# A Mamba-2 scan and a GELU MLP on one NeuronCore: two units share one stretch of scan matmuls, inter-chunk output in 32x64 tiles, stage 1 in 512 columns

## The chip, the cores and the metric

The kernel runs on one core of one Trainium2 chip. The metric is the device time of one execution in microseconds (us). Three runs of the kernel before are given. The profile is one further execution, recorded instruction by instruction.

The engines are named as the profile does: PE is TensorE (matmul), PEld its weight loads, DVE VectorE, ACT ScalarE, POOL GpSimd, and SPq the queue of SyncE, which here issues nearly all DMAs.

## The reference

There are 4 sequences (batch) of 8 heads, 768 tokens, head dimension 32 and state size 16. The scan is computed in chunks; the result goes token by token (3072 tokens of 256 features) through a two-layer MLP.

```python
cum = np.cumsum(log_a, axis=-1)                       # within a chunk
M = einsum('bhin,bhjn->bhij', C, B) * exp(cum_i - cum_j) * causal
y_intra = einsum('bhij,bhjd->bhid', M, x)
y_inter = einsum('bhin,bhnd->bhid', C, state) * exp(cum)
y = y_intra + y_inter
state = exp(sum log_a) * state + sum_j exp(cum_last - cum_j) * B_j x_j
...
h = y.reshape(3072, 256) @ w_in                       # 256 -> 2048
g = 0.5 * h * (1 + tanh(c * (h + 0.044715 * h**3)))
out = g @ w_out                                       # 2048 -> 256
```

## The kernel before

The kernel uses chunks of 128 tokens: 6 for each sequence, 24 in all (`gc`). Two chunks make a unit `u` of 256 tokens, so there are 12 units, three for each sequence. Inputs are cast to bf16, and the decays are folded into B and C ahead of the matmuls, so `bh` is the scaled B transposed (16 state rows of 8 heads, 128 partitions), `ch` the scaled C transposed, and `ce` two copies of `ch` in which the odd or the even heads are zeroed.

For each unit the program has these steps, by the names that the order uses:

- `G` (L614): C·B for all head pairs of both chunks, 8 matmuls in 32-row by 128-column tiles of the PE array, into the PSUM tiles `ga` and `gb`. `M.u.0` and `M.u.1` (L627) multiply them by the causal mask on DVE.
- `D` (L644): the chunk's contribution to the state, 16 matmuls in 128x32 tiles of 64 columns each (8 where a chunk is the last of its sequence). `S` (L692) adds it to the decayed state, `SP` (L704) makes a bf16 copy `sp_new` spread over a block diagonal. Both are on DVE.
- `Y` (L657): the output, 128x32 tiles, 128 columns. A chunk takes 8 matmuls for the inter-chunk part (L673, `sp_new` times `ce`; the first chunk of a sequence has none) and 8 for the intra-chunk part (L682). `yev` copies it to `xm` in SBUF, by ACT or DVE.
- `s1.u.i` (L723): stage 1 of the MLP in 8 steps, each 4 matmuls of 256 columns (two blocks of 128 features, contraction 256 in two halves) into one PSUM bank. `gelu.u.i` on ACT takes it into `gT`.
- `s2.u.k.q` (L740): stage 2 for chunk `k` in four steps of 4 matmuls of 256 columns each. `oev` copies the result out of PSUM, `store` sends it to memory.

PSUM has eight banks: two each for `ga` and `gb`, one for `yb` (Y), one for `o_ps` (stage 2), two for `hp` (stage 1, `D`, small things), taken in turn.

There is no scheduler at work in the build: the string `ORDERED` is the order in which all steps are issued, and each engine runs its own part of it in that order. A suffix `:A`, `:D`, `:P` names the engine of a step that can run on several. From unit 3 on, `Y.u`, `D.u+1` and `G.u+1` are one step. `~n` are warm-up matmuls on zeros.

Loads: `x` by unit (`load_x`, cast by `castx`), B and C by sequence (`load_bc`, scaled by `mul`). Sequence 0 is laid out by steps of its own. Sequence 1 is transposed on PE (`T`, `N`). Sequences 2 and 3 go through memory: `load_wr` writes the scaled bf16 values, `load_tr` reads them back transposed (`bh`, `ch`), `load_bn` reads them plain; `F` makes `ce` from `ch`. The lines of interest of the DMA queue are L170 (`load_bc`), L177 (`load_x`), L513 (`load_wr`), L520 (`load_tr`), L525 (`load_bn`) and L760 (`store`). All DMAs but the first few loads of `a` follow each other on SPq in the written order.

Of the kernel before, what the change touches and what calls it, by code (L numbers as in the profile page):

```python
# [8 lines left out]
FP32 = mybir.dt.float32  # L9
# [5 lines left out]
XL = 6  # L15
# [15 lines left out]
s2.0.0.1.o wo.2.0 wo.2.1:D s1.2.2 gelu.2.1 s2.0.1.1.o D.3 G.3 S.3.0 gelu.2.2 s1.2.3 gelu.2.3 S.3.1
M.3.0 M.3.1 load_wo.3 load_x.4 wo.3.0:A s2.0.0.2.o s2.0.1.2.o wo.3.1 SP.6 s1.2.4 s1.2.5 castx.4.None
s2.0.0.3.o s2.0.1.3.o gelu.2.4 gelu.2.5 oev.0:D s1.2.6 Y.3 oev.1 yev.3.0.2:D s2.1.0.0.o s2.1.0.1.o
s2.1.0.2.o gelu.2.6 s2.1.0.3.o s1.2.7 S.4.0 oev.2 recip.3 S.4.1 s1.3.0 s2.1.1.0.o M.4.1 s2.1.1.1.o
gelu.3.0 s2.1.1.2.o gelu.2.7 s2.1.1.3.o s1.3.1 s1.3.2 gelu.3.1 gelu.3.2 oev.3:D s2.2.0.0.o
s2.2.0.1.o s1.3.3 gelu.3.3 s2.2.0.2.o load_bc.2.1 load_bc.2.0 s2.2.0.3.o mul.2.1:P s1.3.4 M.4.0
load_x.5 s1.3.5 gelu.3.4 mul.2.0:P castx.5.None:D SP.7 oev.4:D SP.8 SP.9 s2.2.1.0.o s2.2.1.1.o
gelu.3.5 s2.2.1.2.o s1.3.6 s2.2.1.3.o gelu.3.6 Y.4 load_wr.2.1 s1.3.7 oev.5:D s2.3.0.0.o yev.4.0.2
load_x.6 load_wr.2.0 S.5.0 gelu.3.7 s1.4.0 s2.3.0.1.o M.5.0 load_tr.2.1 gelu.4.0 SP.10 M.5.1 s1.4.1
s2.3.0.2.o castx.6.None s1.4.2 load_bn.2 gelu.4.1 load_tr.2.0 s1.4.3 store.0 s2.3.0.3.o gelu.4.2  # L40
s1.4.4 gelu.4.3 store.2 F.2 load_x.7 oev.6:D Y.5 s2.3.1.0.o S.6.0 gelu.4.4 yev.5.0.2:D S.6.1
s2.3.1.1.o s1.4.5 gelu.4.5 s2.3.1.2.o load_bc.3.1 s2.3.1.3.o store.1 oev.7 s1.4.6 s1.4.7 s2.4.0.0.o
mul.3.1 load_bc.3.0 store.3 gelu.4.6 load_x.8 castx.7.None load_wr.3.1 gelu.4.7 s2.4.0.1.o s1.5.0
store.4 gelu.5.0 s1.5.1 load_x.9 s2.4.0.2.o M.6.1 M.6.0 gelu.5.1 SP.12 s2.4.0.3.o s1.5.2 oev.8:D
mul.3.0 castx.8.None gelu.5.2 s1.5.3 gelu.5.3 s2.4.1.0.o Y.6 S.7.0 load_wr.3.0 yev.6.0.2 s1.5.4
s2.4.1.1.o gelu.5.4 S.7.1 SP.13 s1.5.5 s2.4.1.2.o s2.4.1.3.o gelu.5.5 oev.9:D SP.15 s1.5.6 s1.5.7
# [38 lines left out]
def kernel(  # L85
# [32 lines left out]
    AL = 2 * Q  # L118

# [8 lines left out]
    GT_BUFS = 5  # L128
# [873 lines left out]
```

## Time and profile before

| | |
|---|---|
| three runs | 116.52, 116.56 (median), 116.89 us |
| span of the profiled execution, first to last instruction | 115.0 us |
| time of the profiled execution itself | not recorded beside its span; the median of the runs is 1.56 us above the span |
| busy: PE, PEld, DVE, ACT, POOL | 108.1, 91.7, 68.0, 70.0, 25.9 us |
| granted PE clock | 1.000 |
| DMA | 16.00 MB, 139 GB/s over the span |

The span is the part of the time that the engines' instructions cover. What lies around it is start and end of the execution. A busy PE is not the same as a PE at its peak, since matmuls overlap: the profile gives each a duration of 0.2 to 0.3 us, while ends follow each other every 0.11 us. Rates are therefore read from the chain of waits, which lists by how much each group pushed the end on, and not from the busy time.

### The profile page before, as it was taken

Reading aid. Unit: us, or ns where it says so; the run is one execution under the profiler, and the core shown is the slowest. Engines: PE = TensorE matmul, PEld = TensorE weight load, DVE = VectorE, ACT = ScalarE, POOL = GpSimd, SP = SyncE. Lnnn points to the kernel's source line nnn. Section 1 sums busy time; section 2 is a strip of 40 time slices with the busy share of each in tenths; the row PEclk is TensorE's granted clock in tenths of the full one; section 3 lists DMA queues with packets and bytes.
Section 4 is the critical chain, followed back from the end, with each engine's and each line's share of the span. In section 5 each row is a group of like instructions: output and inputs, shape, how many; then the busy total and the mean of one; then the engine's idle time right before and its main releaser. Section 6 shows DMA issues by size and latency. Waiting matters only on the chain.

```text
span 115.0 us, 3377 instructions
## 1 busy us (share of the span) xinstructions
PE 108.1 (94%) x1421; PEld 91.7 (80%) x1421; DVE 68.0 (59%) x136; ACT 70.0 (61%) x133; POOL 25.9 (23%) x54
## 2 busy tenths in 40 slices
PE   6979888999999999999999999999999999999990
PEld 2235566888879997989989899889898898999970
DVE  6889998989974755969448491186750851010100
ACT  3159687687654455747675876456495576758620
POOL 7636856806439020201120030000000000000000
PEclk9999999999999999999999999999999999999999
DMA  0999979979994779997556922350003020001113
GB/s 24 231 309 336 332 212 191 317 132 321 215 238 101 141 177 203 196 272 175 88 131 150 209 62 85 111 86 0 0 9 134 0 71 26 0 0 55 42 62 120
DMA packets 43103, 16.00 MB, mean 139 GB/s; under 512 B 36688, under 2 KB 41552, under 8 KB 43088
## 3 DMA queue, kind: packets, MB, share of 16 engines
q1 hardware_dynamic: 42896, 15.70, 55.3%
q8 instruction: 11, 0.18, 0.7%
q10 hardware_dynamic: 192, 0.09, 0.3%
q14 instruction: 4, 0.03, 0.1%
HBM read 11.07 MB, written 3.93 MB: 130 GB/s over the span
## 4 chain that ended last, share of the span: by engine, by line
PE 82%; DVE 5%; DMA 4%; SPq 3%; issue 2%; ACT 2%; DVEq 0%
PE hp L732 35%; PE o_ps L750 34%; DMA x_t<-in_x_dram 4%; PE yb L750 3%; PE yb L673 3%; PE ga L618 2%; PE yb L682 2%; DVE m L628 1%; DVE sp_new L706 1%; SPq L164 1%; ACT gT L736 1%; SPq L151 1%; SPq L160 1%; DVE rt L364 1%; DVE r_t L354 1%
## 5 line engine op out<-in xcount | busy, mean ns | idle before, releaser
L736 ACT ACTIVATE gT<-hp 128x512 bf16<-128x512 f32 x96 | 54.3, 596 | 28.9 <-PE hp L732 28.6
L732 PE MATMUL hp<-xm,w_in_sb 128*128 128x256 bf16 x384 | 53.4, 273 | 1.1 <-DVE s_new L699 0.5
L750 PE MATMUL o_ps<-w_out_sb,gT 128*128 128x256 bf16 x352 | 46.8, 273 | 0.0
L732 PEld LDWEIGHTS <-w_in_sb 128*128 128x128 bf16 x384 | 41.2, 114 | 4.0 <-issue 2.7
L750 PEld LDWEIGHTS <-gT 128*128 128x128 bf16 x384 | 37.4, 98 | 4.1 <-issue 0.4
L341 DVE COPY o_sb<-o_ps 128x256 f32<-128x256 f32 x12 | 5.1, 425 | 26.9 <-PE o_ps L750 26.9
L628 DVE TENSOR_TENSOR m<-ga,tri 128x1024 bf16<-128x1024 f32 x12 | 14.6, 1216 | 0.0
L628 DVE TENSOR_TENSOR m<-gb,tri 128x1024 bf16<-128x1024 f32 x11 | 13.4, 1216 | 0.0
L339 POOL CAST x<-x_t 128x512 bf16<-128x512 f32 x8 | 6.0, 756 | 28.1 <-DMA x_t<-in_x_dram 24.4
L706 DVE SCALAR_TENSOR_TENSOR sp_new<-s_new,pend,bmask 128x256 bf16<-128x256 f32 x17 | 8.0, 483 | 0.1
L699 DVE SCALAR_TENSOR_TENSOR s_new<-s_new,pend,hp 128x64 f32<-128x64 f32 x13 | 3.5, 272 | 7.4 <-PE hp L651 7.3
L720 PE MATMUL yb<-wz 128*128 128x512 bf16 (+2 forms) x21 | 6.6, 455 | 1.1 <-DVE warm L226 1.1
L337 ACT ACTIVATE o_sb<-o_ps 128x256 f32<-128x256 f32 x10 | 3.8, 383 | 5.1 <-PE o_ps L750 3.8
L682 PE MATMUL yb<-m,x 128*32 128x128 bf16 x192 | 6.1, 220 | 0.0
L337 ACT ACTIVATE xm<-yb 128x512 bf16<-128x512 f32 x8 | 4.8, 596 | 1.3 <-PE hp L651 0.7
L720 PEld LDWEIGHTS <-wz 128*128 128x128 bf16 x21 | 2.3, 116 | 4.1 <-issue 2.1
L673 PE MATMUL yb<-ce,sp_new 128*32 128x128 bf16 x160 | 5.3, 221 | 0.0
L339 POOL CAST w_out_sb<-wf 128x512 bf16<-128x512 f32 x6 | 4.1, 692 | 4.7 <-DMA wf<-in_moe_w_out_dram 4.7
L618 PE MATMUL ga<-ce,bh 32*128 32x256 bf16 x48 | 4.7, 273 | 0.3 <-DVE par L289 0.3
L618 PE MATMUL gb<-ce,bh 32*128 32x256 bf16 x48 | 4.7, 273 | 0.0
L750 PE MATMUL yb<-w_out_sb,gT 128*128 128x256 bf16 x32 | 4.5, 273 | 0.0
L682 PEld LDWEIGHTS <-x 128*32 128x32 bf16 x192 | 3.7, 96 | 0.9 <-issue 0.9
(114 smaller groups left out, 75.0 us busy)
## 6 DMA issues: line engine op xcount, KB each, us to landing
out_dram<-o_sb SPq DMA_DIRECT2D x24, 128.0 KB, 2.0
x_t<-in_x_dram SPq DMA_DIRECT2D x20, 128.0 KB, 3.9
wf<-in_moe_w_in_dram SPq DMA_DIRECT2D x4, 512.0 KB, 7.0
wf<-in_moe_w_out_dram SPq DMA_DIRECT2D x4, 512.0 KB, 7.1
bc_t<-in_C_dram SPq DMA_DIRECT2D x3, 384.0 KB, 4.7
bc_t<-in_B_dram SPq DMA_DIRECT2D x3, 384.0 KB, 5.7
scr<-bc SPq DMA_DIRECT2D x4, 192.0 KB, 2.3
x_t<-in_x_dram SPq DMA_DIRECT2D x1, 512.0 KB, 4.4
```

What stands on the lines that cost most here:

```text
L337: nc.scalar.activation(o, i, AF.Copy)
L339: nc.gpsimd.tensor_copy(out=o, in_=i)
L341: nc.vector.tensor_copy(out=o, in_=i)
L618: nc.tensor.matmul(out=gbank(g)[:, 256 * k:256 * k + 256], lhsT=bh_of(2 * u + k)[gs], rhs=ce_of(2 * u + k)[gs], start=True, stop=True, til ...
L628: nc.vector.tensor_tensor(out=m_of(u)[:, 2 * i:2 * i + 2].rearrange("p g k e t -> p (g k e) t"), in0=gx[i].rearrange("p g (k t) -> p (g k) ...
L673: nc.tensor.matmul(out=y4[32 * j:32 * j + 32, k, w], lhsT=sp[:, 32 * h:32 * h + 32], rhs=ce_of(gc)[:, h % 2], start=first(j), stop=False, ...
L682: nc.tensor.matmul(out=y4[32 * j:32 * j + 32, k, w], lhsT=X16[u][:, k, 32 * h:32 * h + 32], rhs=m[:, h // 2, h % 2, :], start=first(j), st ...
L706: nc.vector.scalar_tensor_tensor(out=sp_new.rearrange("p (g d) -> p g d", g=4), in0=(XN[0][:, H * D:H * D + 64] if gc == 0 else state[("s" ...
L720: nc.tensor.matmul(out=t[:, 0:m * 128], lhsT=wz, rhs=w3.to_broadcast([128, m, 128]), start=True, stop=True, skip_group_check=True)
L732: nc.tensor.matmul(out=hp[:, j * T:(j + 1) * T], lhsT=w_in_k[:, w, q, k], rhs=xm[:, w, u * T:(u + 1) * T], start=(w == 0), stop=(w == 1))
L736: nc.scalar.activation(gts[u][:, 2 * i:2 * i + 2], hps.pop((u, i)).rearrange("p (j t) -> p j t", j=2), AF.Gelu_apprx_tanh)
L750: nc.tensor.matmul(out=ops[gc], lhsT=gts[u][:, fi, k * Q:(k + 1) * Q], rhs=w_out_sb[:, fi, :], start=(fi == 0 and (u > 0 or k == 0)), stop ...
```

## The change

1. **Two units, one stretch.** From unit 4 on, `Y` is divided into `Yi` (intra, 128x32 tiles) and `YI` (inter), and units 4-5, 6-7, 8-9 and 10-11 each run them together: `Yi.u Yi.u+1`, then `YI.u YI.u+1`, with the `D` of the next two units and the `G` of one of them beside. The `G` of odd units (5, with `D.5`; 7, 9, 11) stands alone between MLP steps. Each pair's output fills two whole banks, one for each half of the features; `yew` copies them to `xm`, one on ACT and one on DVE.
2. **Inter Y in 32x64 tiles.** `YI` takes 4 matmuls for a chunk instead of 8: contraction 32 (two heads of 16 states), 64 output rows, unmasked `ch`. Tiles 0 and 1 write the two halves of one bank, tiles 2 and 3 those of another. From unit 6 on `G` is in 32x64 tiles too, 16 matmuls instead of 8.
3. **Stage 1 in 512 columns.** From unit 4 on one step takes one block of 128 features for both units: 2 matmuls of 512 columns in place of 4 of 256. `gT` has two buffers for a pair each.
4. **Banks by step.** The four banks a, b, o and y may each hold stage 1, stage 2, `D` or Y; `@` in the order names them.
5. **GpSimd held.** `hold.4` is a copy of one column of `sp_new` of chunk 4 on GpSimd, which stands ahead of `mul.1.1` there.
6. **A new order** of all steps from `Y.0` on, engines of some copies included; some dependencies of `load_tr`, `load_bn` and `mul` are stated more narrowly.

The built instruction lists show it so: PE has 2566 instructions (matmuls and weight loads, with one branch) instead of 2838.

```diff
 ORDERED = """
...
-load_x.5 s1.3.5 gelu.3.4 mul.2.0:P castx.5.None:D SP.7 oev.4:D SP.8 SP.9 s2.2.1.0.o s2.2.1.1.o
-gelu.3.5 s2.2.1.2.o s1.3.6 s2.2.1.3.o gelu.3.6 Y.4 load_wr.2.1 s1.3.7 oev.5:D s2.3.0.0.o yev.4.0.2
...
+castx.2.None:P bn1:D s1.1.0 SP.3
+recip.1 ce1.0:A G.2 D.2 gelu.1.0 s1.1.1 gelu.1.1 S.2.0 SP.4 s1.1.2 wo.0.0:P s2.0.0.0 gelu.1.2 M.2.1
+load_bc.1.1 s1.1.3 gelu.1.3 hold.4 s2.0.1.0 load_bc.1.0 mul.1.1:P M.2.0 s1.1.4 s1.1.5 load_wo.1 load_x.3
+mul.1.0:P gelu.1.4 gelu.1.5 Y.2 s1.1.6 T.1.0 s1.1.7
...
+gelu.3.2 G.5 load_tr.2.1 gelu.3.3 D.5 SP.8 s2.2.0.1 S.5.0 s1.3.4
...
+load_bn.2 s1.3.5 s1.3.6 oev.4:A castx.6.None:D load_tr.2.0 load_bc.3.1 SP.10 load_bc.3.0 s2.2.1.0@o
+s2.2.1.1 gelu.3.5 M.5.1 F.2 s1.3.7 load_x.8 s2.2.1.2 gelu.3.6 gelu.3.7 Yi.4@ya Yi.5 YI.4 YI.5 D.6@b D.7
+G.6 yew.4.0 yew.4.1 s2.2.1.3 S.6.0 S.6.1 S.7.0 s1.4.0@a S.7.1 s2.3.0.0@y gelu.4.0 M.6.0 s1.4.1@b s1.4.2@a
+oev.5:A mul.3.1:D gelu.4.1 gelu.4.2 s1.4.3@o gelu.4.3 s2.3.0.1 s2.3.0.2 s1.4.4@a s1.4.5@b gelu.4.5
+s2.3.0.3 gelu.4.4 s1.4.6@o gelu.4.6 M.6.1 G.7 mul.3.0:P oev.6:D SP.12 castx.8.None:P s1.4.7@b s1.4.8@a
+SP.14 M.7.0 s2.3.1.0@o gelu.4.7 gelu.4.8 s1.4.9@b s1.4.10@y gelu.4.9 load_wr.3.1 s2.3.1.1 load_wr.3.0
+gelu.4.10 s1.4.11@b s1.4.12@a store.3 load_x.9 s2.3.1.2 M.7.1 s1.4.13@y load_tr.3.1 load_bn.3 load_tr.3.0
+load_x.10 s2.3.1.3 gelu.4.11 gelu.4.12 oev.7:D castx.9.None:A s1.4.14@a store.7 gelu.4.13 s1.4.15@b
+s2.4.0.0@o s2.4.0.1 gelu.4.14 load_x.11 gelu.4.15 SP.13 Yi.6@ya Yi.7 D.8@b D.9 G.8 YI.6 YI.7 yew.6.0
...
+gelu.6.15 s2.6.0.1 Yi.8@ya Yi.9 D.10@b D.11 YI.8 YI.9 G.10
...
+gelu.8.15 Yi.10@ya Yi.11 YI.10 YI.11 yew.10.0
...
-s2.11.0.2.yb s2.11.0.3.yb s2.11.1.0.o s2.11.1.1.o s2.11.1.2.o store.19 s2.11.1.3.o oev.22 oev.23
-store.22 store.21 store.18 store.23
+s2.11.0.2 s2.11.1.0@b s2.11.1.1 s2.11.1.2 store.19 s2.11.1.3 store.21 s2.10.0.1
+s2.10.0.2 oev.23:D s2.11.0.3 store.23 s2.10.0.3 oev.20:A store.18 store.20 oev.22:A store.22
 """
...
+    def f_hold(c):
+        nc.gpsimd.tensor_copy(out=held, in_=state[("sp", c)][:, 0:1])
+
     def f_G(u):
+        if u > U2 + 1:
+            for k in range(2):
+                for i, g in [(i, g) for i in range(2) for g in range(4)]:
+                    gs, js = slice(32 * g, 32 * g + 32), slice(64 * i, 64 * i + 64)
+                    nc.tensor.matmul(out=gbank(g)[js, 256 * k:256 * k + 256], lhsT=bh_of(2 * u + k)[gs, js],
+                                     rhs=ce_of(2 * u + k)[gs], start=True, stop=True,
+                                     tile_position=(32 * g, 64 * i), skip_group_check=True)
+            return
...
+    def f_Yi(u):
+        v = u % 2
+        YT[u] = (take("y"), take("o")) if v == 0 else YT[u - 1]
+        for w, k, j in [(w, k, j) for w in range(2) for k in range(2) for j in range(4)]:
+            h, t = 4 * w + j, v * T + k * Q
+            nc.tensor.matmul(out=YT[u][w][32 * j:32 * j + 32, t:t + Q],
+                             lhsT=X16[u][:, k, 32 * h:32 * h + 32], rhs=MT[u][:, h // 2, k, h % 2],
+                             start=(v == 0 and k == 0), stop=True, tile_position=(0, 32 * j), skip_group_check=True)
+
+    def f_YI(u):
+        for k in range(2):
...
+            for g in range(4):
+                gs, i = slice(32 * g, 32 * g + 32), g % 2
+                nc.tensor.matmul(out=YT[u][g // 2][64 * i:64 * i + 64, t:t + Q],
+                                 lhsT=sp[gs, 64 * g:64 * g + 64], rhs=ch_of(gc)[gs], start=False, stop=True,
+                                 tile_position=(32 * g, 64 * i), skip_group_check=True)
+
+    def f_yew(u, w, eng):
+        copy(eng, xm[:, w, u * T:u * T + PT], YT[u][w])
...
+        else:
+            q, k = divmod(i, 4)
             for w in range(2):
...
+                nc.tensor.matmul(out=hp, lhsT=w_in_k[:, w, q, k], rhs=xm[:, w, u * T:u * T + PT],
+                                 start=(w == 0), stop=(w == 1))
```

More of the change, by code (lines that the diff above doesn't have):

```diff
@@ L41 @@
[L41 to L46, printed above, removed]
@@ L322, with take @@
     gx = [ps1.tile([128, 2, 512], FP32, name=f"g{i}") for i in "ab"]
[L323 removed]
+    bank = {k: ps1.tile([128, 512], FP32, name=f"bank_{k}") for k in "aboy"}
+    yb = bank["y"]
+    at = []
+    hp_turn = []
+    def take(pool):
+        if at:
+            return bank[at.pop(0)]
+        if pool == "hp":
+            hp_turn.append(0)
+            return bank["ba"[len(hp_turn) % 2]]
+        return bank[pool]
     y4 = yb.rearrange("p (c w t) -> p c w t", c=2, w=2)
```

262 lines of the change are left out of this document (145 added, 117 removed).

## The prediction

> **What bounds the kernel now.** I read the page's slices first, then the busy time in stretches, then the chain of waits in order of time.
>
> ```profile
> 20.70:49.66 28.96, 28.96 (x380) 25.64 (x383) 22.04 (x38) 17.64 (x32) 10.24 (x12) 1.00 0.90 206
> 49.66:111.94 62.28, 62.26 (x804) 56.02 (x804) 27.93 (x48) 38.96 (x73) 2.60 (x3) 1.00 0.31 77
> 111.94:115.00 3.06, 0.00 (x0) 0.00 (x0) 0.00 (x0) 0.38 (x1) 0.00 (x0) 1.00 0.37 130
> ```
>
> After the stretch come its length and the busy time of PE, PEld, DVE, ACT and POOL, then granted clock, DMA share and GB/s. From 20.70 to 111.94 us PE is never idle, at full clock, while DVE and ACT have room, above all in the second half. So only PE work taken away there shortens the kernel; ahead of it lies a head of 20.7 us, behind it a tail of 3.06 us. The chain (start, us added to the end, what) gives the true price of PE work, at its end and around unit 5:
>
> ```profile
> 108.87 1.31 PE yb L750 x12
> 110.18 1.76 PE o_ps L750 x16
> 111.94 0.02 issue
> 111.96 0.38 ACT o_sb L337
> ```
>
> ```profile
> 49.22 0.44 PE hp L732 x4
> 49.66 0.23 PE yb L673 x8
> 49.88 0.11 PE yb L682 x8
> 49.99 0.11 PE yb L673 x8
> 50.11 0.11 PE yb L682 x8
> 50.22 0.06 PE hp L651 x8
> 50.28 0.21 PE ga L618 x2
> 50.49 0.01 PE gb L618 x2
> 50.50 0.10 PE ga L618 x2
> 50.60 0.01 PE gb L618 x2
> 50.61 0.98 PE o_ps L750 x8
> ```
>
> Twelve MLP matmuls of 256 columns add 1.31, so 0.1092 each and 0.437 for a step of four. Eight Y matmuls in 128x32 tiles add 0.113 by their starts: two rounds of four side by side, 0.057 a round. `D` takes 0.06, `G` two rounds of 0.11. Each time the shape of the tiles changes, about 0.115 comes on top: 0.23 for the first eight of Y, 0.21 for the first of G, 0.98 instead of 0.87 on the way back. Y, D and G take 1.06 us together, and 0.34 of it are three changes of shape.
>
> **Part by part: inter Y.** Y.4 to Y.11 have 16 chunks, two of them (12 and 18, first of their sequences) without an inter part. For 14 chunks two rounds (0.113) become four matmuls in 32x64 tiles. If the four run side by side that is one round, and 14 x 0.057 = 0.79 us is saved. That row tiles overlap shows here:
>
> ```profile
> 9.68 0.20 PE L596 MATMUL o_ps<-x4b,bc0s 32*32 32x64 bf16 x1
> ...
> 9.80 0.19 PE L596 MATMUL hp<-x4b,bc0s 32*32 32x64 bf16 x1
> ```
>
> These are the first and the last of 32 matmuls of 64 columns, over two groups of rows and four of columns, all started within 0.12 us, 4 ns apart. But there different row groups write different banks, while in `YI` tiles 0 and 1 share one. No row shows that. The bounds: one round saves 0.79; two rounds (tile 1 beside tile 2) save nothing; four one after the other cost 14 x (0.227 - 0.113) = 1.59 - 0.79 more, so a loss of 0.79. I take one round, by the nearest row: other rows and other columns of the array. The Trainium skill, "TensorEngine Tiling (Array Packing)", section "Gotcha 1: PSUM Pressure", says that different row tiles cannot access the same PSUM bank at once; by that the saving is lost or reversed. Its page "PSUM — Partial Sum Buffer" (Terms, Quadrant) reports that different 32-partition quadrants of one bank may be accessed at the same time, which speaks for one round.
>
> **Changes of shape**, counted from Y.3 on. Before: eight stretches of three, and Y.11 with two: 26. After: G.4-Y.3-D.4 three; G.5-D.5 three; the stretch of units 4-5 five (into Yi, YI, D, G, back, since D stands between YI and G); those of 6, 8 and 10 three each; G.7, G.9 and G.11 two each: 26. So the sharing itself saves nothing. G in 32x64 tiles has twice the tiles of half the width, still two rounds: nothing, or up to 0.11 a unit (six units, 0.66) if 16 weight loads don't keep up; at the 4 ns above they do.
>
> **512 columns.** 256 matmuls become 128.
>
> ```profile
> 9.92 1.09 PE L720 MATMUL yb<-wz 128*128 128x512 bf16 x5
> ```
>
> ```profile
> L720 PE MATMUL yb<-wz 128*128 128x128 bf16 x1 | 0.2, 219 | 0.0
> ```
>
> These five are four of 512 columns and one of 128: (1.09 - 0.219) / 4 = 0.218 us each, against 2 x 0.1092 = 0.2184. The row is good to some 0.0025 each, so 128 of them give a gain of 0.05, between a gain of 0.35 and a loss of 0.25. I take 0.05. The weight loads that go were hidden under matmuls.
>
> **The head.**
>
> ```profile
> 19.68 0.62 POOL L339 CAST x<-x_t 128x512 bf16<-128x512 f32 x1 [0.68 <-DMA x_t<-in_x_dram]
> ...
> 21.46 1.50 POOL L499 TENSOR_TENSOR bc<-bc_t,pt 128x768 bf16<-128x768 f32 x1 [0.39 <-DVE sp_new L706]
> ```
>
> ```profile
> 20.70 0.60 PE L732 MATMUL hp<-xm,w_in_sb 128*128 128x256 bf16 x4
> ...
> 24.90 0.50 PE L508 MATMUL ga<-ident,bc 128*128 128x128 bf16 x6
> ```
>
> The new order moves G.1 ahead of stage 1 and puts small DVE steps and casts otherwise. Yet by s1.1.1 (20.70) the same PE steps have to be done, and D.2 just before it needs castx.2, whose load lands at 19.68 in the same queue order: no change, 0.2 either way. `hold.4` stands on POOL ahead of mul.1.1, mul.1.0, wo.1.0 and castx.3, and T.1.0 on PE (24.90) waits for both muls. But mul.1.1 was released by an sp_new before too, at 21.46. Now mul.1.0 takes POOL's 1.50 after it: 21.5 + 3.0 = 24.5. Cost nothing; with SP.4 later than 21.9, that lateness.
>
> **The tail.**
>
> ```profile
> 6.32 0.72 ACT L337 ACTIVATE ce<-hp 128x256 bf16<-128x256 bf16 x2 [3.08 <-PE hp L449]
> ```
>
> ```profile
> 110.67 2.03 SPq L760 DMA_DIRECT2D out_dram<-o_sb  x4
> ```
>
> Before, one eviction (0.38) and one store follow the last matmul. After, s2.10.0.3 is last; `oev.20` waits for it, and `oev.22`, whose matmuls ended 0.44 earlier, is queued behind it on ACT. Two evictions in a row take 0.72 (the row of two of 256 columns), so the last store is released 0.34 later, and its issue (2.03 / 4 = 0.5) falls some 0.1 behind that of store.20. Cost 0.45, between 0.34 and 0.6.
>
> **What is late next.** With PE full, the rest of the order is worth nothing unless something arrives late. Evictions fit: behind `YI` PE has G and at least 0.44 of stage 2 before s1 needs `xm`, and `yew` is of a gelu's size. The tightest is sequence 3.
>
> ```profile
> L736 ACT ACTIVATE gT<-hp 128x512 bf16<-128x512 f32 x96 | 54.3, 596 | 28.9 <-PE hp L732 28.6
> ```
>
> ```profile
> 41.66 1.23 SPq L520 DMA_TRANSPOSE bh<-scr  x1
> ...
> 48.62 2.61 SPq L177 DMA_DIRECT2D x_t<-in_x_dram  x2
> ...
> 60.95 0.57 SPq L525 DMA_DIRECT2D bn<-scr  x1
> ```
>
> ```profile
> x_t<-in_x_dram SPq DMA_DIRECT2D x20, 128.0 KB, 3.9
> ...
> bc_t<-in_B_dram SPq DMA_DIRECT2D x3, 384.0 KB, 5.7
> ```
>
> D.9 now stands in the stretch of units 6-7. At 50.61, 64 MLP steps were done; 82 precede Yi.6: 50.61 + 18 x 0.437 = 58.5, plus about 0.6 for D.7, G.7, the way back and two more changes less the saving so far: 59.1 us. D.9 needs bn.3, not even issued before 60.95 until now, and x.9, whose cast stands on ACT ahead of two gelus that empty the banks of Yi.6. In the new order bc.3 follows tr.2.0 (41.66 + 1.23, and two issues: 43.7), lands 5.7 later at 49.4, mul.3.0 on POOL (1.50) ends at 50.9, its write and a store take two issues (1.0), x.9 one to 2.6, and it lands 3.9 after issue: 56.8 to 58.4. Cast and two gelus (3 x 0.6) free the bank at 58.6 to 60.2, and 59.3 is needed. I take no stall; the upper end is 0.9.
>
> **The sum.** -0.79 - 0.05 + 0 (shapes, head) + 0.45 = -0.39 on the span of 115.0: 114.61. The median of the runs is 1.56 above the span of the profiled execution; the same added gives 116.17, rounded 116.15. A measurement of this kernel can tell 0.3% (0.35 us) from no change, so faster begins at 116.21, slower at 116.91.
>
> **Rivals.** (1) *The loads of sequence 3 are late*, the one on the other side: PE stands at Yi.6 or D.9, and the kernel is slower once the stall passes 0.39 + 0.35 = 0.74 us. For it: a slack between +0.7 and -0.9, and a DMA share of 0.90 up to 49.66. Against it: x.6 and x.7 move forward, so the queue is emptier behind. A stall of 1.2 gives 117.35. Chance 0.25. (2) *No overlap in one bank*: two rounds give 116.15 + 0.79 = 116.95, four 117.75. For it the shared bank (by the skill's rule above it would be so), against it the starts 4 ns apart. Chance 0.10. (3) *Handovers in the stretches*: Y takes both banks that the MLP would use, and if the two `yew`, or the four S in a row behind a pair's D, are 0.25 late in each of four stretches, 117.15. Against it: DVE is busy 27.93 of 62.28. Chance 0.12. (4) *Changes into and out of 32x64 tiles are cheaper*: 16 of the 26 involve that shape, which no row shows; at half price 0.92 goes: 115.25. Chance 0.08. That the change doesn't do what it says has no chance of its own: the built lists show 2566 instead of 2838 instructions on PE, as the counts want.
>
> **How the numbers follow.** The forecast has 0.45. Its own range is 115.6 (columns 0.35, tail 0.34, head 0.2 the good way) to 116.6, with 0.33 below 116.21 and 0.12 above. Faster: 0.33 + 0.08 = 0.41. Within 0.3%: 0.12, with 0.04 of (1), 0.05 of (2) and 0.02 of (3): 0.23. Slower: 0.36. The range takes in the forecast, half of (4) and the rivals up to a stall of 1.2: 115.4 to 117.4.
>
> **What would show it.** In the chain after: four matmuls of `YI` in 0.057 once the shape is there; eight s1 matmuls of 512 in 1.74; 0.115 at each of 26 changes; the first idle PE after 20.7, if any, at Yi.6 or D.9 with a DMA or the cast of x.9 as releaser; two evictions of 0.72 behind the last matmul. It is wrong if PE waits in every stretch, if s1.1.1 is more than 0.3 from 20.70, or if a chunk of `YI` takes 0.11 or more.

## The result, and the profile after

The changed kernel is slower by about 1%: 118.19 us (median of 20 runs) beside 116.86 us for the kernel before (20 runs); the ratio is 1.0098, 95% interval 1.0073 to 1.0124. Ratios, here and below, leave out executions more than 1.5% above the fastest of the same kernel, so they are not exactly the quotient of the medians, and of `best3` below only two executions are left. The forecast was 116.15 against 116.56, so it had the wrong sign. The profiled execution took 118.0 us. Its span is 115.95 us in the trace (printed 116.0), against 115.03 before (printed 115.0): 0.92 more.

The span is not the whole time. In the 20 runs of the changed kernel the time is 2.00 to 2.14 us above the span, 2.07 on average; in the runs of the kernel before whose span is on record it is 1.66 to 1.78, 1.71 on average. So 0.36 of the loss lies outside the span, ahead of the first instruction or behind the last, where the profile shows nothing.

In the names of the changed kernel `G` is L644 (L637 in 32x64 tiles), `D` L679, `Yi` L721, `YI` L734, stage 1 L790 (L795 in 512 columns), stage 2 L816, `T` L519, the muls L510, copies L348 (ACT), L350 (POOL) and L352 (DVE). Both kernels have done the same PE work when `G.3` begins, so I divide the span there. First the busy time in stretches of the kernel after (stretch, its length, then busy time of PE, PEld, DVE, ACT, POOL, granted clock, DMA share, GB/s):

```profile
20.72:29.64 8.92, 8.42 (x120) 7.19 (x117) 7.26 (x13) 5.74 (x11) 5.48 (x7) 1.00 0.96 258
29.64:49.00 19.36, 19.16 (x288) 16.02 (x281) 16.64 (x33) 9.84 (x20) 4.22 (x5) 1.00 0.94 194
49.00:112.32 63.32, 63.31 (x650) 44.08 (x648) 27.79 (x48) 37.83 (x72) 3.22 (x3) 1.00 0.30 73
112.32:116.00 3.68, 0.00 (x0) 0.00 (x0) 0.00 (x0) 0.66 (x2) 0.00 (x0) 1.00 0.32 110
```

and the same cut of the kernel before:

```profile
20.70:28.81 8.11, 8.11 (x114) 7.22 (x114) 7.40 (x12) 6.16 (x11) 3.85 (x6) 1.00 0.95 253
28.81:111.94 83.13, 83.11 (x1072) 74.44 (x1064) 42.57 (x74) 50.45 (x95) 8.99 (x10) 1.00 0.45 104
```

The reader is to see three pieces. The head, up to `G.3`, is 0.83 longer (29.64 against 28.81). From `G.3` to PE's end the kernel is 0.45 shorter (19.36 + 63.32 = 82.68 against 83.13). The tail is 0.54 longer (3.63 against 3.09; the stretches of 3.68 here and 3.06 in the prediction end at the rounded spans). The sum is the 0.92 of the spans.

The gain in the middle is where it was forecast. The chain of waits of the kernel after, around the first pair:

```profile
46.35 0.11 PE bank_a L721 x8
46.46 0.17 PE bank_y L734 x2
46.63 0.01 PE bank_a L734 x2
46.64 0.05 PE bank_y L734 x2
46.69 0.01 PE bank_a L734 x2
46.70 0.05 PE bank_y L734 x2
46.75 0.01 PE bank_a L734 x2
46.75 0.05 PE bank_y L734 x2
46.80 0.01 PE bank_a L734 x2
46.81 0.23 PE bank_b L679 x16
47.04 0.23 PE ga L637 x2
```

A chunk of `YI`, four matmuls in two banks, adds 0.06 (0.05 + 0.01); the first pays 0.12 more for the change of shape. Two row tiles thus do work into one bank at once. The rule of the Trainium skill, "TensorEngine Tiling (Array Packing)", section "Gotcha 1: PSUM Pressure", that they cannot, does not hold for this pair of tiles, which write different quadrants (groups of 32 partitions). The Trainium skill, "PSUM — Partial Sum Buffer" (Terms, Quadrant), reports that different quadrants of one bank may be accessed at the same time; the trace agrees, with 0.06 a chunk.

The losses show in the same chain, in the head, at unit 3 and behind the pairs:

```profile
16.44 6.20 DMA bc_t<-in_C_dram
22.71 2.96 POOL bc L510 x2
25.71 0.51 PE ga L519 x6
...
33.90 0.29 ACT o_sb L348
34.21 0.44 DVE o_sb L352
34.69 0.60 PE bank_o L816 x4
...
48.80 0.57 PE bank_b L795 x2
49.37 0.43 PE bank_a L795 x2
...
77.62 0.51 PE bank_a L795 x2
78.13 0.43 PE bank_b L795 x2
```

`T.1.0` (25.71) waits for the second mul on GpSimd. `s2.1.0.0` (34.69) waits for both `oev` of unit 0, one behind the other, on the bank it takes: 0.20 of idle. And behind three of the four pairs one of the first stage 1 steps adds 0.51 to 0.57 instead of 0.43 (two of them are shown).

### The profile page after: what moved, and what is told of

Its sections match the earlier page's. It is cut to its first block, busy times and chain, and to the rows that moved or that the text cites. A ratio compares the mean times of both kernels' runs of the same rounds, so it can differ in the third digit from the quotient of the medians.

```text
span 116.0 us, 3122 instructions
## 1 busy us (share of the span) xinstructions
PE 107.9 (93%) x1285; PEld 77.3 (67%) x1285; DVE 68.8 (59%) x143; ACT 67.0 (58%) x128; POOL 25.5 (22%) x53
## 4 chain that ended last, share of the span: by engine, by line
PE 73%; SPq 10%; DMA 9%; POOL 3%; ACT 1%; issue 1%; ACTq 0%; DVE 0%
PE bank_o L816 19%; PE bank_y L816 14%; PE bank_b L795 10%; PE bank_a L795 10%; DMA bc_t<-in_C_dram 5%; SPq L154 4%; DMA bcf<-in_B_dram 4%; PE bank_a L790 3%; PE bank_b L790 3%; SPq L194 3%; POOL bc L510 3%; PE bank_o L795 2%; PE ga L637 2%; PE bank_a L816 2%; PE bank_b L816 2%; PE bank_y L795 1%
## 5 line engine op out<-in xcount | busy, mean ns | idle before, releaser
L816 PEld LDWEIGHTS <-gT 128*128 128x128 bf16 x384 | 37.0, 98 | 11.0 <-issue 1.0
L816 PE MATMUL bank_o<-w_out_sb,gT 128*128 128x256 bf16 x208 | 29.0, 273 | 0.2 <-DVE o_sb L352 0.2
L804 ACT ACTIVATE gT<-bank_a 128x512 bf16<-128x512 f32 x27 | 16.1, 596 | 11.3 <-PE bank_a L795 11.2
L816 PE MATMUL bank_y<-w_out_sb,gT 128*128 128x256 bf16 x144 | 19.2, 273 | 0.0
L795 PEld LDWEIGHTS <-w_in_sb 128*128 128x128 bf16 x128 | 14.0, 114 | 7.5 <-DVE xm L352 0.4
L804 ACT ACTIVATE gT<-bank_b 128x512 bf16<-128x512 f32 x27 | 16.0, 594 | 2.9 <-PE bank_b L795 2.8
L795 PE MATMUL bank_a<-xm,w_in_sb 128*128 128x512 bf16 x54 | 16.1, 380 | 0.0
L795 PE MATMUL bank_b<-xm,w_in_sb 128*128 128x512 bf16 x54 | 16.1, 379 | 0.0
L790 PEld LDWEIGHTS <-w_in_sb 128*128 128x128 bf16 x128 | 13.5, 114 | 2.4 <-POOL w_in_sb L350 0.9
L801 ACT ACTIVATE gT<-bank_a 128x512 bf16<-128x512 f32 x17 | 10.1, 595 | 8.3 <-PE bank_a L790 8.3
L352 DVE COPY o_sb<-bank_y 128x256 f32<-128x256 f32 x6 | 2.5, 422 | 15.0 <-PE bank_y L816 10.6
L801 ACT ACTIVATE gT<-bank_b 128x512 bf16<-128x512 f32 x15 | 9.0, 597 | 3.9 <-PE bank_b L790 3.8
L790 PE MATMUL bank_a<-xm,w_in_sb 128*128 128x256 bf16 x68 | 10.2, 273 | 0.0
L790 PE MATMUL bank_b<-xm,w_in_sb 128*128 128x256 bf16 x60 | 9.1, 274 | 1.0 <-ACT xm L348 0.6
L350 POOL CAST x<-x_t 128x512 bf16<-128x512 f32 x7 | 4.6, 652 | 18.4 <-PE bank_a L795 11.3
L773 PE MATMUL bank_y<-wz 128*128 128x512 bf16 (+2 forms) x21 | 6.8, 462 | 1.1 <-DVE warm L225 1.1
L352 DVE COPY o_sb<-bank_o 128x256 f32<-128x256 f32 x9 | 3.8, 421 | 6.1 <-PE bank_o L816 3.2
L352 DVE CAST xm<-bank_a 128x512 bf16<-128x512 f32 x4 | 2.8, 690 | 5.7 <-PE bank_a L734 5.6
```

The lines of the kernel that those rows point to most:

```text
L350: nc.gpsimd.tensor_copy(out=o, in_=i)
L352: nc.vector.tensor_copy(out=o, in_=i)
L773: nc.tensor.matmul(out=t[:, 0:m * 128], lhsT=wz, rhs=w3.to_broadcast([128, m, 128]), start=True, stop=True, skip_group_check=True)
L790: nc.tensor.matmul(out=hp[:, j * T:(j + 1) * T], lhsT=w_in_k[:, w, q, k], rhs=xm[:, w, u * T:(u + 1) * T], start=(w == 0), stop=(w == 1))
L795: nc.tensor.matmul(out=hp, lhsT=w_in_k[:, w, q, k], rhs=xm[:, w, u * T:u * T + PT], start=(w == 0), stop=(w == 1))
L801: nc.scalar.activation(gts[u][:, 2 * i:2 * i + 2], hp.rearrange("p (j t) -> p j t", j=2), AF.Gelu_apprx_tanh)
```

## Experiments

In the table, "G.3" and "middle" (from there to PE's end) are from each profile, and "median G.3" is the median span of the runs in the ratio less the middle and the tail of its own profile. That column holds only as far as the middle is the same in all runs of a kernel. "Outside" is the mean of time less span over all runs of the kernel.

| kernel | median us | ratio (interval) | G.3 | middle | tail | median G.3 | outside |
|---|---|---|---|---|---|---|---|
| before, in all sets | 116.9 to 117.3 | 1 | 28.81 | 83.13 | 3.09 | 28.9 to 29.2 | 1.71 |
| before_again | 117.34 (one run) |  | 29.41 | 83.12 | 3.11 |  | 1.74 |
| the change | 118.19 | 1.0098 (1.0073 to 1.0124) | 29.64 | 82.68 | 3.63 | 29.8 | 2.07 |
| after_again | 118.09 | 1.0080 (1.0042 to 1.0118) | 29.34 | 82.72 | 3.64 | 29.5 | 2.08 |
| mul_on_dve | 118.30 | 1.0086 (1.0049 to 1.0124) | 29.86 | 82.67 | 3.64 | 29.8 | 2.10 |
| no_hold | 118.48 | 1.0127 (1.0068 to 1.0186) | 30.03 | 82.67 | 3.63 | 30.0 | 2.08 |
| tail_order | 117.28 | 1.0032 (0.9995 to 1.0069) | 29.68 | 82.68 | 3.20 | 29.7 | 1.72 |
| head_early | 117.97 | 1.0089 (1.0045 to 1.0133) | 29.94 | 82.67 | 3.66 | 29.6 | 2.06 |
| head_full | 118.47 | 1.0145 (1.0081 to 1.0209) | 29.38 | 83.70 | 3.65 | 29.2 | 1.97 |
| inter_128x32 | 118.70 | 1.0151 (1.0081 to 1.0221) | 29.80 | 83.19 | 3.65 | 29.8 | 2.09 |
| stage1_256 | 119.47 | 1.0155 (1.0063 to 1.0246) | 30.45 | 83.28 | 3.64 | 29.9 | 2.09 |
| handovers | 118.25 | 1.0107 (1.0066 to 1.0148) | 29.29 | 83.07 | 3.64 | 29.3 | 2.05 |
| x_first | 118.44 | 1.0110 (1.0064 to 1.0155) | 30.16 | 82.67 | 3.64 | 30.0 | 2.06 |
| all_fixed | 117.41 | 1.0040 (1.0012 to 1.0068) | 29.30 | 82.68 | 3.16 | 29.4 | 2.06 |
| head_G3 | 118.00 | 1.0084 (1.0053 to 1.0114) | 28.73 | 82.70 | 3.66 | 29.5 | 2.05 |
| before_new_head | 117.72 | 1.0039 (1.0003 to 1.0075) | 29.18 | 83.11 | 3.09 | 29.7 | 1.72 |
| best | 117.21 | 0.9977 (0.9944 to 1.0010) | 29.32 | 82.75 | 3.16 | 29.1 | 2.07 |
| best2 | 117.85 | 1.0074 (1.0043 to 1.0105) | 28.96 | 83.51 | 3.17 | 29.1 | 2.07 |
| best2_no_held | 118.15 | 1.0087 (1.0045 to 1.0129) | 29.03 | 83.53 | 3.14 | 29.1 | 2.06 |
| best3 | 118.56, 118.63 (two runs) |  | 28.95 | 84.74 | 3.16 |  | 1.71 |

best3 has no interval. The last column takes one of two values, near 1.71 and near 2.06 (head_full 1.97), whatever the head. tail_order and best3 have the lower one although the rest of the changed kernel is in them, and best, whose last steps are those of best3, has the higher one. So no edit tried here says what sets it: the 0.36 is measured, its origin stays open. A ratio between kernels of different groups holds some 0.35 us that no step in the span explains.

**The change once more, and a second profile of before.** Both without an edit.

> The changed kernel once more, for a second profile. Theory: the 1.0 us more of span is made of PE waiting at T.1.0 for the two scalings of sequence 1 on GpSimd (0.8), PE waiting for two evictions of one bank behind Y.3 (0.2), handovers in the stretches (0.4) and a longer tail (0.6), less 1.1 that inter Y and 512 columns save; so the same waits show again, T.1.0 at about 25.7 us. Rival: the waits at T.1.0 come from a DMA that landed late in that one execution; then T.1.0 stands elsewhere by 0.5 us or more and the span with it. Ratio to the kernel before: 1.010.

> The kernel before, profiled once more, to see how far its head differs from one execution to the next. Theory A, the new order of the head costs: D.2 starts within 0.3 us of its 20.35 and T.1.0 within 0.4 us of its 24.90. Rival, the profile of before caught an early landing of its x: D.2 starts at 20.9 us or later with the x cast behind its transfer, as in the profiles of the changed kernel.

In after_again `T.1.0` stands at 25.43 and PE does not wait there, so the wait of 0.50 did not come again; waits of 0.42, 0.42 and 0.24 stand earlier instead (below). In before_again the sign that the rival named came: `D.2` started at 21.06 instead of 20.35, its x cast at 20.40 instead of 19.68, behind its transfer. `D.2` on PE, first in the profile of before, then in before_again:

```profile
20.35 0.21 PE L651 MATMUL hp<-x,bn 128*32 128x64 bf16 x4
```

```profile
21.06 0.21 PE L651 MATMUL hp<-x,bn 128*32 128x64 bf16 x4
```

The middle repeats to 0.05 in eight profiles that share its order (82.67 to 82.72) and to 0.01 in the two of before, while `G.3` moves by 0.6 from one execution of the same kernel to the next. So the head has to be judged by many runs, not by one profile; by "median G.3" the new one costs about 0.6 (29.5 and 29.8 against 28.9 to 29.2).

**The muls on GpSimd, and the hold.** In mul_on_dve `mul.1.0:P` becomes `mul.1.0:D`; in no_hold the step `hold.4` is left out.

> The changed kernel with mul.1.0 on DVE, as it was before, and nothing else. Theory (two scalings of 1.5 us in a row on GpSimd hold T.1.0): mul.1.0 runs on DVE right after M.2.0, T.1.0 starts at its place in the order, about 25.0 instead of 25.7, and the kernel is 0.6 to 0.8 us faster than the changed one: ratio to before about 1.003. Rival (the load of B and C of sequence 1 lands late, so the engine does not matter): less than 0.3 us is gained and DVE or PE waits for the DMA at the same place.

> The changed kernel without hold.4 on GpSimd. Theory: GpSimd is released at 22.0 by the held copy but the load of C lands only at 22.7, so nothing changes (within 0.2 us of the changed kernel). Rival (the held copy is what makes T.1.0 late): mul.1.1 starts up to 0.7 us earlier and the kernel gains 0.5 us or more.

Neither gains: 1.0086 and 1.0127. With the second mul on DVE, `T.1.0` has no wait in its profile and stands at 25.95, later than 25.71: PE was already late in front of it. The wait of the first profile was a symptom.

**The tail.**

```diff
-s2.10.0.2 oev.23:D s2.11.0.3 store.23 s2.10.0.3 oev.20:A store.18 store.20 oev.22:A store.22
+s2.10.0.2 oev.23:D store.18 s2.11.0.3 oev.22:D store.23 s2.10.0.3 oev.20:A store.22 store.20
```

> The changed kernel with another order of its last steps: oev.22 on DVE right behind s2.11.0.3, store.18 ahead, store.22 before store.20. Theory: one eviction and one store follow the last matmul, as before the change; the tail goes from 3.7 to about 3.1 us, so 0.5 us faster than the changed kernel (0.3 to 0.6). Rival (the landing of the last stores, two at once, sets the end): under 0.2 us.

The ratio falls by 0.0066 (0.8 us) against the first runs of the changed kernel and by 0.0048 (0.6 us) against after_again, which ran beside it. By the profiles 0.44 of it is the tail (3.20 against 3.64), as forecast; some 0.35 more lies outside the span, where no theory had looked for it. ACT at the end, first of the change, then of tail_order:

```profile
112.34 0.38 ACT L348 ACTIVATE o_sb<-bank_o 128x256 f32<-128x256 f32 x1 [6.33 <-PE bank_o L816]
112.62 0.38 ACT L348 ACTIVATE o_sb<-bank_a 128x256 f32<-128x256 f32 x1
```

```profile
112.45 0.38 ACT L348 ACTIVATE o_sb<-bank_o 128x256 f32<-128x256 f32 x1 [6.38 <-issue]
```

The second eviction behind the last matmul is gone, and with it the late last store.

**The two savings, undone one at a time.** inter_128x32 forms `YI` in eight 128x32 matmuls from `ce`; stage1_256 splits each stage 1 step into four matmuls:

```diff
-            for g in range(4):
-                gs, i = slice(32 * g, 32 * g + 32), g % 2
...
+            for w, j in [(w, j) for w in range(2) for j in range(4)]:
+                h = 4 * w + j
+                nc.tensor.matmul(out=YT[u][w][32 * j:32 * j + 32, t:t + Q],
+                                 lhsT=sp[:, 32 * h:32 * h + 32], rhs=ce_of(gc)[:, h % 2], start=False, stop=True,
```

```diff
-                nc.tensor.matmul(out=hp, lhsT=w_in_k[:, w, q, k], rhs=xm[:, w, u * T:u * T + PT],
+                for v in range(2):
+                    nc.tensor.matmul(out=hp[:, v * T:(v + 1) * T], lhsT=w_in_k[:, w, q, k],
+                                     rhs=xm[:, w, (u + v) * T:(u + v + 1) * T],
```

> The changed kernel with the inter Y from unit 4 in eight matmuls of 128x32 tiles for a chunk, as the kernel before forms it, in place of four of 32x64. If four 32x64 tiles go in one round though two of them write one bank: 14 chunks by 0.057 us more, 0.8 us, less two or three shape changes of 0.115 us that fall away: 0.5 us over the changed kernel, ratio 1.011 to 1.014. If the small tiles had saved nothing: ratio 1.008 to 1.009, as the changed kernel.

> The changed kernel with each stage 1 step of units 4 to 11 in four matmuls of 256 columns in place of two of 512. From the steps of both profiles (0.430 to 0.434 against 0.437 us, 64 steps): 0.2 to 0.45 us over the changed kernel, ratio 1.010 to 1.0125. If the forecast's 0.05 us is right: no difference, 1.008 to 1.009.

By the middle of their profiles the small tiles are worth 0.52, net of the changes of shape that go with them, and the 512 columns 0.60. The ratios, 1.0151 and 1.0155, point the same way, with intervals too wide to size them.

**The order of the head.** head_early has the old order up to `s1.1.1`, head_G3 up to `G.3`, head_full up to `s1.2.7`; before_new_head is the other way round, the kernel before with the new order up to `G.3`. The part of the new order that matters for DVE, against the old:

```diff
-XX.1 XD.1 wi.1.0 tp2 wi.2.1 xn.2 s1.0.0 G.1 S.1.0 s1.0.1 xn.3 gelu.0.0 gelu.0.1 s1.0.2 gelu.0.2
-M.1.1 wi.2.0 M.1.0 s1.0.3 gelu.0.3 s1.0.4 s1.0.5 recip1 S.1.1 gelu.0.4 gelu.0.5 SP.1 load_wi.3
+wi.1.1:P S.1.0 SP.1 wi.2.1:P G.1 xn.2:A M.1.0 SP.2 M.1.1 tp2 s1.0.0 gelu.0.0 load_wi.3 s1.0.1 gelu.0.1
+s1.0.2 s1.0.3 recip1 gelu.0.2 gelu.0.3
```

> The changed kernel with the order of the kernel before up to and with s1.1.1 of unit 1 (the same steps; the rest keeps the new order). Theory A, the loss of the head comes from VectorE's new order, in which SP.1, M.1.0, SP.2 and M.1.1 stand ahead of tp2, recip1 and pe, so that T1, N1, G.2 and D.2 wait: T1 starts by 17.9 us again, s1.1.1 by 20.9 us, and the time falls by 0.3 to 0.7 us against the changed kernel, ratio to before 1.003 to 1.006. Rival B, the loss lies behind s1.1.1, where the second sequence's T.1.0 stands: ratio stays at 1.008 to 1.010 with T.1.0 at 25.4 us or later.

> The changed kernel with the order of the kernel before up to and with s1.2.7 of unit 2 (the same steps; hold.4 stands ahead of mul.1.0), so that the new head is undone whole and units 4 to 11 and the tail stay. Theory A, the head's order costs about 1.1 us, the savings of the stretches 1.14 us, their handovers 0.44 us and the tail 0.6 us: the time is 116.7 to 117.0 beside a before of 116.9, ratio 0.998 to 1.001, and no wait of 0.2 us ahead of s2.1.0.0. Rival, the ledger of one profile misleads and the head is even: ratio 1.006 or more.

> The changed kernel with the order of the kernel before up to and with G.3 of unit 3 (where both kernels have done the same work of TensorE), hold.4 ahead of mul.1.0, and the new order behind it. Theory E, the order of the head costs the 0.6 us: G.3 comes at 29.1 us at the median, 82.7 us from there to TensorE's end, the tail as it is: 0.5 us under the changed kernel, ratio 1.003 to 1.006. Rival F, it is not the order (transfers, the held tile, the layout of memory): ratio 1.008 to 1.010.

> The kernel before with the changed kernel's order up to G.3 of unit 3, without hold.4, and its own order, stretches and tail behind it. Theory E: the new order of the head alone costs 0.5 to 0.7 us here too, ratio 1.004 to 1.006, with 83.1 us from G.3 to TensorE's end. Rival F: ratio 0.999 to 1.002.

What the new order does is seen on PE. First after_again, then before_new_head:

```profile
18.42 0.29 PE L478 MATMUL gb<-ident,bc0s 128*128 128x128 bf16 x2 [0.42 <-POOL bc0s L470]
...
19.62 0.28 PE L498 MATMUL ga<-ident,bh 128*128 128x128 bf16 x2 [0.42 <-DVE bh L352]
...
20.58 0.28 PE L644 MATMUL ga<-ce,bh 32*128 32x256 bf16 x2 [0.24 <-DVE bn L352]
```

```profile
18.14 0.28 PE L467 MATMUL gb<-ident,bc0s 128*128 128x128 bf16 x2 [0.42 <-POOL bc0s L459]
...
19.33 0.28 PE L487 MATMUL ga<-ident,bh 128*128 128x128 bf16 x2 [0.42 <-DVE bh L341]
...
20.29 0.28 PE L618 MATMUL ga<-ce,bh 32*128 32x256 bf16 x2 [0.24 <-DVE bn L341]
```

The same three waits, `T1`, `N1`, `G.2`, come with the order into the other kernel. The last two stand in all nine profiles with the new order, the first in seven, and the set in none with the old. The old order has waits of its own, though: PE waits five times between 12.4 and 17.7 in the profile of before, 1.30 together, where the three make 1.08. So the waits have moved, and the price has to be read from when PE gets there. The reason for the new ones stands on DVE: `tp2`, on which all of them hang, runs at 12.31 in the kernel before and, behind two `sp_new` and two masks, at 16.34 in after_again:

```profile
12.31 0.99 DVE L364 STREAM_TRANSPOSE rt<-r_t 32x64 f32<-32x64 f32 x4
```

```profile
15.10 1.21 DVE L654 TENSOR_TENSOR m<-gb,tri 128x1024 bf16<-128x1024 f32 x1
16.34 0.74 DVE L375 STREAM_TRANSPOSE rt<-r_t 32x64 f32<-32x64 f32 x3
```

The dates bear the price out over all profiles. `s1.1.1` starts at a median of 20.70 in the eleven with the old order up to it (20.36 to 21.30; x_first and all_fixed, which load x.2 earlier, are among them), and of 21.21 in the nine with the new one (20.72 to 22.02). `G.3` starts at a median of 29.0 in the eight with the old order up to `G.3` or beyond (28.73 to 29.41), and of 29.7 in the nine with the new one (29.18 to 30.45). Leave out the three profiles of the kernel before, with either head, and it is 28.73 to 29.38 against 29.29 to 30.45. "Median G.3" says the same: 29.1 to 29.5 with the old order, 29.3 to 30.0 with the new.

The times are less plain. In the kernel before the new order costs 0.0039 (0.0003 to 0.0075), some 0.5 us; that is theory E's value, but the interval holds the rival's 1.002 too. In the changed kernel the old order gives less back: 1.0089 and 1.0084 beside 1.0098 and 1.0080 (head_full's 1.0145 is spoilt by its middle, 83.70). head_early loses again behind `s1.1.1` what it might have won, with 0.74 at `D.2` for the cast of x and 0.27 at `T.1.0`. head_G3, whose interval holds both theory E's 1.006 and the rival's 1.010, does not bear theory E out by itself. best, below, which is head_G3 with the tail and three moves mended, is 0.0055 under tail_order, though their intervals just overlap. So theory E holds for the dates of the head; how much of it reaches the time of the changed kernel is not settled.

**x first.** head_early with `load_x.2` ahead of `load_wo.0`, and `castx.2` ahead of `wo.0.0`.

> The kernel with the old order up to s1.1.1 (head_early), and load_x.2 put ahead of the 512 KB load_wo.0 in SP's queue and castx.2 ahead of wo.0.0 on GpSimd. Theory C, the head has two limits of about the same lateness, VectorE's order and the landing of x for D.2: with both gone D.2 starts by 20.5 us and the time falls by 0.5 to 0.8 us from the changed kernel, ratio 1.003 to 1.005. Rival D, DMA in all is late and the wait moves to w_out, C or B: ratio 1.008 or more, with a wait for a transfer ahead of s2.0.0.0 or T.1.0.

`D.2` came at 19.98, and then `s2.0.0.0` waited 0.76 for the cast of `w_out`. Rival D held: in the head one transfer's gain is the next one's loss.

**Handovers, and all at once.**

```diff
-oev.0:D D.4 S.4.0 s2.1.0.0@o s1.2.7
+oev.0:D D.4 S.4.0 s1.2.7 s2.1.0.0@o
...
-gelu.4.0 M.6.0 s1.4.1@b s1.4.2@a oev.5:A mul.3.1:D gelu.4.1 gelu.4.2 s1.4.3@o gelu.4.3 s2.3.0.1
+gelu.4.0 M.6.0 s2.3.0.1 s1.4.1@b s1.4.2@a oev.5:A mul.3.1:D gelu.4.1 gelu.4.2 s1.4.3@o gelu.4.3
...
-s2.6.0.3 s1.8.0@a gelu.8.0 s1.8.1@b SP.21 gelu.8.1 s2.6.1.0@y
+s2.6.0.3 s2.6.1.0@y s1.8.0@a gelu.8.0 s1.8.1@b SP.21 gelu.8.1
```

and the like for `s2.8.1.0` ahead of `s1.10.0`. all_fixed has these, x_first and the tail of tail_order; best has head_G3, the same tail and the three moves shown. In both `oev.22` stays on ACT, ahead of `oev.20`, where tail_order has it on DVE.

> The changed kernel with four steps of TensorE moved by one place: s1.2.7 ahead of s2.1.0.0 on its bank, s2.3.0.1 ahead of s1.4.1 on bank b, s2.6.1.0 and s2.8.1.0 on bank y ahead of s1.8.0 and s1.10.0. If the short waits at these steps (0.20, 0.14, 0.08 and 0.11 us) are what the new bank order costs: 0.3 to 0.5 us under the changed kernel, ratio 1.004 to 1.007. Rival, the waits only move to the next step: 1.0085 to 1.010.

> x_first with the four moves of handovers and the new order of the tail (tail_order). If the three losses are separate and add up, 0.6 + 0.4 + 0.6 us under the changed kernel's 1.0 us over before: ratio 0.994 to 0.998. If only the tail counts: 1.002 to 1.004.

> head_G3 with the new order of the tail (tail_order) and three of the four moves of handovers (without that of s2.8.1.0, behind which s1.10.3 waited 0.25 us). If the head's order, 0.33 us of handovers and 0.5 us of tail come off: 1.4 us under the changed kernel, ratio 0.994 to 0.998. If the head's order does nothing: 0.999 to 1.002.

The moved waits went, but handovers gained nothing: 1.0107. Its profile has two new waits on PE:

```profile
46.80 0.29 PE L637 MATMUL ga<-ce,bh 32*64 32x256 bf16 x2 [0.35 <-DMA bh<-scr]
...
95.24 0.59 PE L795 MATMUL bank_o<-xm,w_in_sb 128*128 128x512 bf16 x2 [0.25 <-ACT gT L804]
```

The second is of the move of `s2.8.1.0`. The first is `G.6`, which PE reaches before sequence 2's transposed B has landed. all_fixed's 1.0040 is the forecast for the tail alone. best, without the move of `s2.8.1.0`, is the fastest kernel made here, 1.2% under the changed kernel by the ratios; against before its interval holds 1. Its 0.9977 lies within the 0.994 to 0.998 expected if the head's order counts.

**Sequence 2's transfers.** best2 puts `load_x.6` and `load_x.7` behind `load_wr.2.0`, and the cast of x.7 later; best2_no_held is the same without `hold.4` and its tile; best3, shown here, puts them behind `load_tr.2.0`, and `store.1` behind them.

```diff
-M.4.0 load_x.5 load_x.6 load_x.7 s2.1.0.2 load_wr.2.1
+M.4.0 load_x.5 s2.1.0.2 load_wr.2.1
...
-load_wr.2.0 store.1
+load_wr.2.0
...
-castx.6.None:D load_tr.2.0 load_bc.3.1
+load_tr.2.0 load_x.6 load_x.7 store.1 load_bc.3.1
...
+castx.6.None:P castx.7.None:P load_x.8
```

> best with load_x.6 and load_x.7 behind load_wr.2.0 in SP's queue, so that the scratch write and its read-back for sequence 2 come earlier. If the 0.31 us that best waits for bh ahead of G.6 then goes: 82.4 us or less from G.3 to TensorE's end (best 82.75), ratio 0.992 to 0.996. If another transfer takes its place: 0.996 to 0.999.

> best2 without hold.4 and without its tile. If the hold, or the place in memory that its tile takes, costs the rest of the head: G.3 0.2 to 0.3 us earlier by the spans and a ratio 0.002 to 0.003 under best2. Rival, the rest is only the spread of the transfers: the same ratio as best2, or within 0.001 of it.

> best with load_x.6, load_x.7 and store.1 behind the whole read-back of sequence 2 (load_tr.2.1, load_bn.2, load_tr.2.0) in SP's queue, and the casts of those x behind them on GpSimd. Theory G, sequence 2's round trip through memory is the second limit: bh is issued by 42.0 us (best 43.70), G.6 follows D.6 without a wait, at 46.4 us or as much earlier as the head is, and the time falls 0.3 to 0.6 us under best: ratio 0.992 to 0.996. Rival, the read-back only seemed to bound: ratio 0.997 to 1.000, or later x loads make Yi.6 wait.

All three are worse. PE in best, best2_no_held and best3:

```profile
46.82 0.29 PE L637 MATMUL ga<-ce,bh 32*64 32x256 bf16 x2 [0.31 <-DMA bh<-scr]
```

```profile
46.68 0.30 PE L679 MATMUL bank_b<-x,bn 128*32 128x64 bf16 x16 [0.71 <-DMA bn<-scr]
47.31 0.29 PE L637 MATMUL ga<-ce,bh 32*64 32x256 bf16 x2 [0.33 <-DMA bh<-scr]
```

```profile
47.37 0.24 PE L679 MATMUL bank_b<-x,bn 128*32 128x64 bf16 x8 [1.48 <-POOL x L350]
48.27 0.24 PE L679 MATMUL bank_b<-x,bn 128*32 128x64 bf16 x8 [0.67 <-POOL x L350]
```

The issue of `bh` on SP's queue, in the kernel before, in the changed kernel and in best3:

```profile
41.66 1.23 SPq L520 DMA_TRANSPOSE bh<-scr  x1
```

```profile
43.39 1.23 SPq L531 DMA_TRANSPOSE bh<-scr  x1
```

```profile
40.69 1.23 SPq L531 DMA_TRANSPOSE bh<-scr  x1
```

Before, `bh` was issued 8.6 us ahead of `G.6` (50.28 in the chain that the prediction quotes); after, 3.65 us (47.04). It takes 3.1 us to land in best's chain. So the shared stretch of units 4-5 brings `G.6`, and `D.6` and `D.7` beside it, 3 us forward, to where `bn`, `bh`, x.6 and x.7 land through one queue. best3 had `bh` in time, and then waited 2.15 for x. best2_no_held is no faster than best2, so the hold and its tile are not the rest of the head.

## Why the prediction was wrong

- **What bounds the kernel, and inter Y**: right. One round a chunk, 0.06; the forecast took 0.057. The bound for four matmuls one after the other was added up wrongly: 14 x (0.227 - 0.113) is a loss of 1.59 against the kernel before, not 0.79, so rival 2's worst case was 118.5 and not 117.75. It did not come.
- **512 columns**: right in kind, mis-sized. The 0.218 for a matmul of 512 came from a warm-up row; the chain after shows 0.43 for two. Over 64 steps that is 0.2 to 0.45 by the rounding of the rows, 0.60 by stage1_256's middle, not 0.05. The Trainium skill, "TensorE: Matmul & The Clock Gate", section "Wait — 56ns, not 53.3ns?", gives 215.7 ns warm for 512 columns; against the 2 x 0.1092 of the trace that is an estimate of 0.35 for 128 matmuls, nearer to what was measured than the warm-up row.
- **The head: this step failed.** It said that by `s1.1.1` the same PE steps have to be done, hence "no change, 0.2 either way". Equal work was taken for equal time. The new order puts four long DVE steps (`SP.1`, `M.1.0`, `SP.2`, `M.1.1`) and a short one ahead of `tp2`, and PE reaches what hangs on it later: 0.5 at `s1.1.1` by the medians of the profiles, 0.5 us by before_new_head, about 0.6 at `G.3` by the spans. The first profile hid it: there `s1.1.1` stands at 20.72, within the bound that was set for calling the step right, because that execution had an early head and lost its time at `T.1.0`. That it came within the bound was luck.
- **The muls before `T.1.0`**: forecast to end at 24.5; they ended at 25.67, since C landed only at 22.64. But it cost nothing that moving one of them could give back.
- **The tail**: right, 0.54 by the profiles instead of 0.45, within its 0.34 to 0.6.
- **The sum: a second term that was put at nothing.** What lies outside the span was carried over from before ("the same added"). It grew by 0.36, from 1.71 to 2.07 on average. The 1.56 itself came from the median of three runs less the span of another execution. No edit shows why the term grew.
- **What is late next**: the right question with the wrong sequence. Sequence 3 never stopped PE. Sequence 2, whose use moves from 50.28 to 47.04, was not looked at.
- **Rival 3, handovers**: partly there: 0.20 at `s2.1.0.0`, and 0.14, 0.08 and 0.11 at early stage 1 steps behind three pairs, 0.5 in all where the rival had 0.25 in each of four stretches. Of the 0.65 by which the middle fell short of its two savings (1.1 against 0.45), that accounts for 0.5. Rival 4 did not come: the change into the 32x64 tiles of `YI` cost 0.12, as others do.

By the forecast's terms: inter Y and columns about -1.1, handovers and the rest of the middle +0.65, head +0.6, tail +0.54, outside the span +0.36: +1.05. Measured is 1.0098 x 116.86 - 116.86 = 1.15, within 0.85 and 1.45.

What stays open: where the 0.36 outside the span comes from, and why the old head order gives back so little time in head_G3, 0.0014 of the ratio. The edge at `D.6` and `G.6` is a candidate: waits of 0.3 to 2.2 stand there in five kernels whose PE comes early, and none in any profile of before. That it is the cause was not shown, as no order tried had all four transfers clearly in time. all_fixed and head_G3 had no such wait in their profiles, which are single executions.

## What to carry to other kernels

Equal work ahead of a step is not equal time: when an order is rewritten, follow the chain of small steps on the second engine (here four long DVE steps ahead of one transpose) to the matmul that hangs on it. When a change brings a step forward, list all that the step reads and compare the issue of each transfer with the new date, for each sequence, not only for the tightest. Divide the span at steps where both kernels have done the same work: here one piece repeated to 0.05 us, another moved by 0.6 us without any edit, and a single profile of the second could have supported either story. And compare time less span of both kernels before adding the terms up: here 0.36 of the 1.15 lay where no profile looks.

## What the runs showed that was not expected

A DVE step with two inputs in SBUF took twice as long beside GpSimd's casts in one profile. Here is `sp_new` in after_again on DVE, with the casts on POOL:

```profile
12.73 0.92 DVE L759 SCALAR_TENSOR_TENSOR sp_new<-s_new,pendq,bmask 128x256 bf16<-128x256 f32 x1
...
14.70 0.47 DVE L759 SCALAR_TENSOR_TENSOR sp_new<-s_new,pendq,bmask 128x256 bf16<-128x256 f32 x1
```

```profile
12.15 2.53 POOL L350 CAST w_in_sb<-wf 128x512 bf16<-128x512 f32 x4 [1.11 <-DMA wf<-in_moe_w_in_dram]
14.89 1.32 POOL L350 CAST w_in_sb<-wf 128x512 bf16<-128x512 f32 x2 [0.21 <-DMA wf<-in_moe_w_in_dram]
```

The first falls among four casts and takes 0.45 longer than the second, which begins between two groups of them. The Trainium skill, "SBUF — State Buffer", section "SBUF: two separate sides", says that such a DVE step and a GpSimd step that reads SBUF exclude each other for a whole instruction; a cast here is some 0.6, so the trace agrees. It was not tried by itself.
